# Two attention-fed mixture-of-experts layers: the last layer in groups of 512, 256 and 128 rows, and one routing product moved from GpSimd to VectorE

## The chip, the cores and the metric

The kernel runs on one NeuronCore of a Trainium2 chip. The metric is the device time of one execution in microseconds (us), lower is better. TensorE does the matmuls; VectorE (DVE), ScalarE (ACT) and GpSimd (POOL) do the elementwise work; SyncE (SP) issues most of the DMAs, GpSimd the indirect ones, which gather or scatter rows by a list of row numbers. Each engine works through its own list of instructions in order and waits on semaphores for the others.

## The reference

Inputs are q, k, v of shape (4, 8, 576, 64), and the weights of two expert layers. Cut to what matters:

```python
attn = softmax(block-causal mask of q @ k.T / sqrt(64)) @ v       # blocks of 64 positions
x = attn as (2304, 512)                                           # a row is a token
# first expert layer: 8 experts, each token goes to its two best
noisy = x @ w_gate + log1p(exp(x @ w_noise)) * noise
out[t] = sum over the two best e of weight * (relu(x[t] @ w1[e]) @ w2[e])   # 512 -> 1024 -> 512
# second expert layer: each token goes to its best expert alone
logits = out @ w_gate2 + modality_bias[modality_id]
e = argmax(logits); gate = softmax(logits)[e]
y[t] = gate * (relu(out[t] @ v1[e]) @ v2[e])                      # 512 -> 1024 -> 512
```

With the inputs given, the reference sends 1165 tokens of the second layer to expert 1, 1139 to expert 2 and none to the others. 866 and 852 of these do not use expert 7 in the first layer.

## The kernel before, in words

All matrices are float32 split into a high and a low part of a type that TensorE takes in one pass, so that each product is three matmuls: high by high, high by low, low by high. The weights come from memory as `raw` tiles of 128x1024, ScalarE copies the high part (`wh`), and VectorE or GpSimd subtracts it to make the low part (`wl`).

The program has three stages. **Attention** works over 16 pairs of heads. When a batch is complete, a part of the *first routing* (`route`, line 650) follows: it finds the two best experts of each token and makes, with matmuls of 0/1 matrices, the list of row numbers of each expert. `routes` runs it three times: for batches 0 and 1, for batch 2, and for batch 3. In it `hot_a` (line 281) makes the products `sl_ov` of a one-hot matrix with the values to be listed, `hot_b` the other one-hot matrix `sl_ob`, and `lists` (line 296) multiplies the two on TensorE into `pt`. The second run ends in `early(1)` (line 1135), which turns the sums into row numbers (`acc`, `ids`, `idg`) and issues the three gathers `wide<-X,idg` of the first expert-1 job.

The **first expert layer** is a list of jobs (`Job`, line 466). A job gathers tiles of 128 rows (`xr`), transposes them on TensorE into the one PSUM tile `px`, copies high and low parts to `xth` (ScalarE) and `xtl` (VectorE), runs `mm1` (the first matrix, `ph`, 96 matmuls as wide as the job's rows, up to 512) and then per tile of rows `mm2` (the second matrix, `py`, 24 matmuls of 512 columns). The transposes of the next job stand inside `mm2` of the present one. In attention's last microseconds TensorE already runs `mm1` of the first job (expert 0; there its tiles bear the names `ps` and `kh`), and its `mm2` holds the transposes of the expert-1 job, as `px<-ident,wide`. Rows of results are added to `X2`, and dot products with the second layer's gate (`zero<-py`, 8 per tile, VectorE) are added to `LG`.

The **last layer** needs the second routing, `gates(k)` (line 1466). `gates(0)` starts when the rows of experts 0 to 6 are in, and looks only at tokens that are complete by then; `gates(1)` starts when expert 7 is in and takes the rest. Each fills a table of row numbers. A table holds groups of 256 rows of one expert: three for `gates(0)` (`NE`), which takes only full groups, and seven for `gates(1)` (`NS`). Each group is one `Job` with its own load of both weight matrices. If a row finds no place, the flag `more` is 1 and a slow loop behind the list of jobs (line 1593) does what is left.

The order of instructions on TensorE, ScalarE and VectorE is fixed when the program is built. A planner keeps a modelled clock for each engine: during attention it picks the step that can start earliest (`earliest`, line 1316, due times in `SCHED`), and a routing step is let in when the modelled VectorE is free; a product on GpSimd makes the next routing step wait for the modelled GpSimd clock. In the expert stages `run` (line 1407) writes jobs in order and calls due routing steps between matmuls (`beat`, `tick`). Where a gather or a `wl` falls in a job is set there too: `fs` and `eb` say after which quarter of `mm1` a second-layer weight is split, and on which engine.

Of the kernel before, what the change touches and what calls it, by code (L numbers as in the profile page):

```python
# [30 lines left out]
def moe_kernel(tc, q, k, v, w_gate, w_noise, noise, w1, w2, mod_id, w_gate2, mod_bias, m2w1, m2w2, out):  # L31
    nc = tc.nc
    B, H, S, D = q.shape
    NT, DM = out.shape
    E = w_gate.shape[1]
# [3 lines left out]
    NP = CAP // 128  # L39

    FIRST = (2, 3)
    NE = 3
    NV = 5
    NA1 = E * NP
    NTT = NT // 128
    G2 = 256
    NG2 = 16
    NS = 10 - NE
    NA2 = NG2 * G2 // 128
    NQ = 4  # L50
    NY = 3
# [3 lines left out]
    def bc(ap, shape):  # L55
        return ap.to_broadcast(shape)
# [47 lines left out]
    with ExitStack() as top:  # L104
# [18 lines left out]
        def iota(t, pattern, base=0, cm=0):  # L123
            nc.gpsimd.iota(t, pattern=pattern, base=base, channel_multiplier=cm, allow_small_or_imprecise_dtypes=True)
# [34 lines left out]
                            for name, dt in (("ids0", I32), ("idg0", I32), ("gts0", F32)))  # L159
        gts1 = cst.tile([128, NA1], F32, name="gts1")  # L160

        table = [(cst.tile([128, 2 * n], I32, name="ids%d" % i), cst.tile([128, 2 * n], F32, name="gts%d" % i),
                  cst.tile([1, NG2 + 1], I32, name="eg%d" % i)) for i, n in ((2, NE), (3, NS), (4, NG2))]
        eo = cst.tile([1, NG2 + 1], I32, name="eo")
        gso = cst.tile([128, E], F32, name="gso")
        more = cst.tile([1, 1], I32, name="more")
# [22 lines left out]
        def consts2():  # L189
            iota(pad2, [[0, NA2]], base=NT + CAP, cm=1)  # L190
            iota(th2, [[G2, 9]])
            iota(th3, [[G2, 9]], base=G2 - 1)
            iota(th1, [[G2, 7]], base=CAP)
            nc.sync.dma_start(wg2, w_gate2.rearrange("(k p) e -> p k e", p=128))
            nc.sync.dma_start(mid, mod_id.bitcast(I32).rearrange("(p t w) -> p t w", p=128, w=2))
            gps.tensor_copy(midf, mid[:, :, 0])
            nc.sync.dma_start(bias1, mod_bias.rearrange("(o m) e -> o (m e)", o=1))
            nc.gpsimd.memset(one1, 1.0)
            gps.tensor_scalar(vals2[:, :, 0], bc(part, [128, NTT]), 1.0, None, op0=OP.add)
            gps.tensor_copy(vals2[:, :, 1], lane[:, 0:NTT])  # L200
# [265 lines left out]
        class Job:  # L466
# [44 lines left out]
            def mm1(s, f, hp_):  # L511
                wh, wl = (w[:, :, 128 * (f % 2):128 * (f % 2) + 128] for w in s.wa[f // 2])
                h1, h2 = hp_(f, s.n)
                for c0, cn in s.parts:
                    cs = slice(c0, c0 + cn)
                    ph = ps_h.tile([128, 512], F32, name="ph")
                    for kk in range(4):
                        for i, (w, xx) in enumerate(((wh, s.xth), (wh, s.xtl), (wl, s.xth))):
                            ten.matmul(ph[:, 0:cn], w[:, kk], xx[:, kk, cs], start=(kk == 0 and i == 0), stop=(kk == 3 and i == 2))
                        if kk % 2 == 0:  # L520
                            beat()
                    act.activation(h1[:, cs], ph[:, 0:cn], AF.Relu)
# [85 lines left out]
            return Job((w1[e], w2[e]), X1, nt, lambda t: ids1[:, e * NP + t0 + t:e * NP + t0 + t + 1],  # L608
                       lambda t: gts1[:, e * NP + t0 + t:e * NP + t0 + t + 1], add_rows(ids1, e * NP + t0, nt, then), need)

        def group(W1, W2, table, ev, ic, gc, emit, need=(None, None)):
            def w():
                e = ev()
                return W1[bass.ds(e, 1)].rearrange("o d f -> (o d) f"), W2[bass.ds(e, 1)].rearrange("o f d -> (o f) d")
            return Job(w, table, G2 // 128, ic, gc, emit, need)

        prev_out = []
        HG = 4
# [10 lines left out]
        def job2(k, g):  # L629
            ids, gts, eg = table[k]  # L630
            ic = lambda t: ids[:, 2 * g + t:2 * g + t + 1]
            j = group(m2w1, m2w2, X2, lambda: nc.sync.value_load(eg[0:1, g:g + 1], min_val=0, max_val=E - 1), ic,
                      lambda t: gts[:, 2 * g + t:2 * g + t + 1], put_rows(ic), ("eg%d" % k, "ids%d%d" % (k, g >= HG)))
            if k == 0:
                j.apart = last_rows
            return j
# [6 lines left out]
        chain = lambda k, p: lambda: walk(gates(k), now[0] + .5, p)  # L643
        firsts = [job1(0, FIRST[0], NP - FIRST[0], need=(None, "ids1"))]
        firsts += [job1(e, then={E - 2: chain(0, 1), E - 1: chain(1, 1)}.get(e), need=(None, "ids1")) for e in range(2, E)]
        seconds = [job2(0, g) for g in range(NE)] + [job2(1, g) for g in range(NS)]
        stage = Stage([j00, j10] + firsts + seconds)


        def route(b0, nb):  # L650
# [101 lines left out]
            for b in range(nb):  # L752
                n = slice(10 * b, 10 * b + 10)
                ob = yield from hot_b(rt, bl[:, n], 10)
                ov = yield from hot_a(rt, a[:, n], 10, 0, NA1, va[:, n], b0 + nb < B)
                yield from lists(pl, ob, ov, 10, b == 0, b == nb - 1)
            if b0 == 0:
                vec.tensor_copy(acc1, pl)
# [648 lines left out]
        def run(jobs, hp_, ea, eb, nxt=None, stage=stage):  # L1407
# [3 lines left out]
            for n, j in enumerate(jobs):  # L1411
                nx = jobs[n + 1] if n + 1 < len(jobs) else nxt

                def rows():
                    if nx and nx.ready(1) and len(nx.xr) < nx.nt:
                        nx.gather(len(nx.xr))

                for f in range(len(j.hh), NF // 128):
                    j.mm1(f, hp_)
                    if f in fs and len(j.wb) < NQ:  # L1420
                        stage.split(eb[fs.index(f) % len(eb)] if "ids1" in flags else vec)
                    stage.fetch(ah)
                    rows()
                    filler()
                    tick(j.n * .005)
# [40 lines left out]
        def gates(k):  # L1466
# [1 line left out]

            flags.add("chain")
            pool = r2[0]  # L1470
            th = th2 if k else th3
            ids, gts, dst = table[k]
            cap = ids.shape[1]
            sh = [128, NTT, E]
# [27 lines left out]
            n = yield from experts_of(pool, gn, gs, dst, "g_")  # L1502
            flags.add("eg%d" % k)
            if k == 1:

                go, s_ = yield from starts(pool, base, th1, "o_")
                vec.tensor_copy(gso, s_)
                yield .3
                no = yield from experts_of(pool, go, gso, eo, "o_")
                m = pool.tile([1, 1], F32, name="g_m")  # L1510
                vec.tensor_scalar(m, n, -float(NS), 0.0, op0=OP.add, op1=OP.max)
                yield .3
                vec.tensor_add(m, m, no)
                yield .3
                vec.tensor_scalar(more, m, 1.0, None, op0=OP.min)
                yield .3
# [10 lines left out]
            vec.scalar_tensor_tensor(a, st, float(G2 // 128), a, op0=OP.mult, op1=OP.add)  # L1527
            yield .3
            if k == 0:
                vec.tensor_tensor(t0, oh, bc(gn[:, None, :], sh), op=OP.mult)  # L1530
                yield .3
                vec.tensor_reduce(st, t0, axis=AX, op=OP.add)
                yield .3
                vec.scalar_tensor_tensor(msk, st, float(G2), pos, op0=OP.mult, op1=OP.is_gt)
                yield .3

            vec.tensor_scalar(msk, msk, -1e5, 1e5, op0=OP.mult, op1=OP.add)
            yield .3
# [2 lines left out]
            if k < 2:  # L1541
                new = tl("new") if k else placed
                vec.tensor_scalar(new, a, cap - .5, None, op0=OP.is_lt)
                yield .3
                if k:
                    vec.tensor_add(placed, placed, new)
                    yield .3

            vec.tensor_tensor(l, l, bc(mx[:, :, None], sh), op=OP.subtract)
# [26 lines left out]
        with sp():  # L1576
            with tc.tile_pool(name="hp1", bufs=1, reuse_waits="tile") as hp1:
                run([j00, j10, j11] + firsts, hidden(hp1), [gps], [gps], seconds[0])
            hp2 = ph2.enter_context(tc.tile_pool(name="hp2", bufs=1, reuse_waits="tile"))
            with tc.tile_pool(name="ws2", bufs=4, reuse_waits="tile") as ws2:  # L1580
                rings["raw"].add(ws2, 4)
                run(seconds, hidden(hp2), [vec], [vec, gps])
                while heap or fill:
                    if heap:
                        pop()
                    clk["pe"] = max(clk["pe"], clk["dve"], now[0]) + 1
                    filler()
            rings["raw"] = Ring("raw", F32, (wp, 5))
# [119 lines left out]
```

## Time and profile before

Three timed runs gave 990.72, 992.0 and 994.84 us (median 992.0).

| | |
|---|---|
| time of the profiled execution | 991.67 us |
| its span, first to last instruction | 989.9 us |
| mean granted TensorE clock | 0.993 |
| busy: TensorE / weight loads / VectorE / ScalarE / GpSimd | 96% / 87% / 71% / 53% / 53% |
| weight tiles of 512 KB (`raw`) | 144 |
| DMA traffic | 141.6 MB, mean 143 GB/s |

The profiled execution lies 0.3 us below the median, well within the spread, so that its rows can be added up against its own time. A matmul's record is longer than its share of TensorE, because matmuls overlap; the distance between two starts is what one of them costs.

### The profile page before, as it was taken

To read this page: it belongs to the slowest core of one execution; us is meant where nothing else is said; L and a number is where in the kernel's file an instruction comes from. 1 tells how busy PE (TensorE), PEld (TensorE's weight loads), DVE (VectorE), ACT (ScalarE), POOL (GpSimd) and SP (SyncE) were. 2 spreads that over 40 slices of the span, in tenths; PEclk is the share of its full clock that TensorE was granted. 3 is DMA by queue.
4 is the path that set the end of the run, shared out by engine and by line. 5 is a ranking of instruction groups with operands and counts; after the bars stand their busy time and mean duration, and the time that the engine had idled before them with its cause. 6 is when DMAs were issued, how large, how long until landed. Compare 5 with 4: busy or idle time off the path is not lost.

```text
span 989.9 us, 17527 instructions
## 1 busy us (share of the span) xinstructions
PE 949.4 (96%) x6072; PEld 860.7 (87%) x6072; DVE 703.6 (71%) x1707; ACT 520.9 (53%) x1156; POOL 521.0 (53%) x488
## 2 busy tenths in 40 slices
PE   8999998999979999999999999999999899999995
PEld 6989897998868998989899898989979779999994
DVE  6878779888769967386693948669788866555450
ACT  6989997988542344334333333433335535555551
POOL 6234333464423599586685848648476253333321
PEclk9999999999989999999999999999999999999998
DMA  5577752222376377464563727434466877776620
GB/s 127 106 217 197 221 131 65 72 60 68 92 236 197 54 171 181 118 151 107 128 129 93 143 86 150 107 86 54 143 129 195 279 234 233 229 220 219 197 86 12
DMA packets 158258, 141.60 MB, mean 143 GB/s; under 512 B 76233, under 2 KB 124745, under 8 KB 158034
## 3 DMA queue, kind: packets, MB, share of 16 engines
q1 hardware_dynamic: 139042, 106.92, 37.4%
q0 software_dynamic: 18064, 33.23, 16.7%
q8 instruction: 50, 0.82, 0.3%
q14 instruction: 46, 0.38, 0.1%
q10 hardware_dynamic: 1056, 0.26, 0.1%
HBM read 112.54 MB, written 28.36 MB: 142 GB/s over the span
## 4 chain that ended last, share of the span: by engine, by line
PE 73%; DVE 9%; issue 5%; ACT 5%; DMA 4%; POOL 3%; SPq 1%; POOLq 0%; ACTq 0%; DVEq 0%
PE ph L71 28%; PE py L71 27%; PE pt L71 7%; PE ps L71 6%; PE pa L71 3%; PE px L71 2%; DVE wl L71 2%; ACT p L71 2%; POOL wl L71 2%; ACT kp L71 1%; DVE kp L71 1%; DMA xr<-X,ids 1%; DVE nm L71 1%; DVE PTl L71 1%; DMA qld<-in_q_dram 1%
## 5 line engine op out<-in xcount | busy, mean ns | idle before, releaser
L71 POOL TENSOR_TENSOR wl<-raw,wh 128x1024 fp32r<-128x1024 f32 x80 | 207.5, 2623 | 106.4 <-ACT wh L71 92.2
L71 PE MATMUL ph<-xth,wh 128*128 128x320 f32 (+2 forms) x800 | 241.2, 302 | 2.1 <-DVE kp L71 2.1
L71 PE MATMUL ph<-xth,wl 128*128 128x320 f32 (+2 forms) x800 | 240.0, 300 | 0.0
L71 PE MATMUL ph<-xtl,wh 128*128 128x320 f32 (+2 forms) x800 | 240.0, 300 | 0.0
L71 DVE SCALAR_TENSOR_TENSOR zero<-py,gts,wide 128x512 f32<-128x512 f32 x304 | 227.5, 748 | 8.3
L71 PE MATMUL py<-wh,kp 128*128 128x512 f32 x496 | 168.1, 399 | 0.0
L71 PEld LDWEIGHTS ph<-xth,wh 128*128 128x128 f32 x800 | 151.7, 190 | 4.0 <-DVE kp L71 2.8
L71 PEld LDWEIGHTS ph<-xtl,wh 128*128 128x128 f32 x800 | 151.7, 190 | 0.7
L71 PEld LDWEIGHTS ph<-xth,wl 128*128 128x128 f32 x800 | 151.7, 190 | 0.0
L71 ACT ACTIVATE wh<-raw 128x1024 fp32r<-128x1024 f32 x144 | 150.8, 1053 | 0.6 <-DMA raw<-in_moe_w_dram 0.5
L71 ACT ACTIVATE yr<-py,gts 128x512 f32<-128x512 f32 x60 | 41.3, 689 | 147.1 <-PE py L71 104.6
L71 PEld LDWEIGHTS py<-wh,kp 128*128 128x128 f32 x496 | 94.0, 189 | 18.5
L71 DVE SCALAR_TENSOR_TENSOR hl<-ph,hh 128x320 fp32r<-128x320 f32 (+2 forms) x100 | 46.4, 465 | 79.1 <-ACT hh L71 78.9
L71 DVE TENSOR_TENSOR wl<-raw,wh 128x1024 fp32r<-128x1024 f32 x64 | 80.1, 1259 | 29.8 <-ACT wh L71 29.1
L71 PE MATMUL py<-wl,kp 128*128 128x512 f32 x248 | 97.4, 393 | 0.0
L71 PE MATMUL ps<-kh,kp 128*128 128x256 f32 (+5 forms) x320 | 95.7, 340 | 0.6 <-ACT p L71 0.4
L71 POOL DMA_INDIRECT xr<-X,ids x55 | 57.5, 1045 | 73.5 <-PE px L71 44.2
L71 PE MATMUL py<-wh,hh 128*128 128x512 f32 x232 | 94.0, 405 | 0.0
L71 DVE TENSOR_TENSOR xtl<-px,xth 128x512 fp32r<-128x512 f32 x58 | 40.0, 690 | 74.3 <-ACT xth L71 74.3
L71 PE MATMUL py<-wl,hh 128*128 128x512 f32 x232 | 90.6, 390 | 1.7 <-POOL wl L71 1.7
L71 ACT ACTIVATE hh<-ph 128x320 fp32r<-128x320 f32 (+2 forms) x100 | 41.8, 418 | 95.1 <-PE ph L71 91.6
L71 PE MATMUL py<-wh,hl 128*128 128x512 f32 x232 | 90.9, 392 | 0.0
(253 smaller groups left out, 1830.9 us busy)
## 6 DMA issues: line engine op xcount, KB each, us to landing
raw<-in_moe_w_dram SPq DMA_DIRECT2D x144, 512.0 KB, 4.0
X<-zero SPq DMA_DIRECT2D x13, 512.0 KB, 4.2
kld<-in_k_dram SPq DMA_DIRECT2D x32, 128.0 KB, 2.9
vld<-in_v_dram SPq DMA_DIRECT2D x32, 128.0 KB, 2.7
X<-x SPq DMA_DIRECT2D x16, 256.0 KB, 2.6
qld<-in_q_dram SPq DMA_DIRECT2D x30, 128.0 KB, 2.8
wide<-in_moe_w_dram SPq DMA_DIRECT2D x4, 512.0 KB, 6.5
wide<-WG2T POOLq DMA_DIRECT2D x1, 2048.0 KB, 10.2
```

The costliest lines, as they stand in the source:

```text
L71: return f(*a, **kw)
```

## The change

The last layer's groups become 512 rows wide (`GW`), two in each table, and the second table gets two small ones in addition, one of 256 rows and one of 128. `gates(1)` therefore works out, beside the number of full 512-row groups of each expert (`gn`), the groups of 256 that hold the rest (`nr`, `gm`, `gr`, table `egs`). `more` is now worked out from the number of rows placed. In a job of 128 rows `mm1` reads its columns twice, so that a matmul is 256 wide. In the first routing the products of the second run go to VectorE. In the job `firsts[0]` (the rest of expert 0) the last two of four second-matrix splits go to VectorE. The ring of raw weight tiles has 7 in place of 9 in the last layer.

```diff
-    NE = 3
+    GW = 512
+    BW, NW, NSM = GW // 128, 2, 2
...
-            iota(th3, [[G2, 9]], base=G2 - 1)
+            iota(th3, [[GW, 9]], base=GW - 1)
...
-                            ten.matmul(ph[:, 0:cn], w[:, kk], xx[:, kk, cs], start=(kk == 0 and i == 0), stop=(kk == 3 and i == 2))
+                            o, xx = ph[:, 0:cn], xx[:, kk, cs]
+                            if cn == 128:
+                                o, xx = ph[:, 0:2 * cn].rearrange("p (r c) -> p r c", r=2), bc(xx[:, None], [128, 2, cn])
+                            ten.matmul(o, w[:, kk], xx, start=(kk == 0 and i == 0), stop=(kk == 3 and i == 2))
...
-        seconds = [job2(0, g) for g in range(NE)] + [job2(1, g) for g in range(NS)]
+        seconds = [job2(k, g) for k in range(2) for g in range(NW)] + [job2(1, g, True) for g in range(NSM)]
...
-                ov = yield from hot_a(rt, a[:, n], 10, 0, NA1, va[:, n], b0 + nb < B)
+                ov = yield from hot_a(rt, a[:, n], 10, 0, NA1, va[:, n], b0 == 0)
...
+                eb_ = [gps, gps, vec, vec] if j is firsts[0] else eb
...
-                        stage.split(eb[fs.index(f) % len(eb)] if "ids1" in flags else vec)
+                        stage.split(eb_[fs.index(f) % len(eb_)] if "ids1" in flags else vec)
...
             if k == 1:
-
+                nr = pool.tile([128, E], F32, name="g_nr")
+                vec.scalar_tensor_tensor(nr, gn, -float(GW), pp[:, NTT], op0=OP.mult, op1=OP.add)
+                yield .3
+                gm, gr = yield from starts(pool, nr, th2, "q_")
+                yield from experts_of(pool, gm, gr, egs, "q_")
...
+                    ten.matmul(pm, ones, held, start=True, stop=True)
...
+                    vec.tensor_scalar(more, m, float(NT) - .5, None, op0=OP.is_lt)
...
-            with tc.tile_pool(name="ws2", bufs=4, reuse_waits="tile") as ws2:
-                rings["raw"].add(ws2, 4)
+            with tc.tile_pool(name="ws2", bufs=2, reuse_waits="tile") as ws2:
+                rings["raw"].add(ws2, 2)
```

The planner then writes another order. All that follows up to the second routing run is the same in both. **First place: VectorE at the end of attention**, where that run makes its lists. `kp<-ps` are the low parts of the first job's hidden rows, `kld` and `qld` halves of its weights. Before:

```order
L71 TENSOR_TENSOR sl_oa<-lane,sl_a_3856 128x400
L71 SCALAR_TENSOR_TENSOR kp_3954<-ps,kp_3954 128x256
L71 TENSOR_TENSOR wl<-kld,wh 128x512
L71 TENSOR_TENSOR wl<-qld,wh 128x512
L71 SCALAR_TENSOR_TENSOR kp_3954<-ps,kp_3954 128x256
L71 SCALAR_TENSOR_TENSOR kp_4041<-ps,kp_4041 128x256
```

and now:

```order
L71 TENSOR_TENSOR sl_oa<-lane,sl_a_3857 128x400
L71 SCALAR_TENSOR_TENSOR kp_3955<-ps,kp_3955 128x256
L71 TENSOR_TENSOR sl_ov<-sl_oa,vals 128x1000 x2
L71 TENSOR_TENSOR wl<-kld,wh 128x512
L71 TENSOR_TENSOR wl<-qld,wh 128x512
L71 SCALAR_TENSOR_TENSOR kp_3955<-ps,kp_3955 128x256
L71 TENSOR_TENSOR acc_98<-acc_98,pt 128x200
```

The two products are new on VectorE, and the sum `acc`, which stood behind all eight `kp` and all four pairs of `wl`, now stands behind two `kp` and one pair. Between it and `idg` stand two `kp` and one pair of `wl` that were ahead of it. On TensorE the ten `pt<-sl_ov,sl_ob` stood behind the last of the 96 `ps<-kh` and `ps<-kl` matmuls of the first job; now three stand behind 24 of these and seven behind 36, so that 60 come after them. The four `sl_ov` are gone from GpSimd's list, and its three gathers `wide<-X,idg` stand behind the same work as before.

**Second place: TensorE at the start of the last layer**, the end of expert 7's `mm2` and the first `mm1` of the last layer. Before:

```order
L71 MATMUL py<-wh,hl_8193 128x512
L71 MATMUL py<-wh,hh_8258 128x512
L71 MATMUL py<-wl,hh_8258 128x512
L71 MATMUL py<-wh,hl_8259 128x512
L71 MATMUL ph<-xth,wh 128x256
L71 MATMUL ph<-xtl,wh 128x256
```

and now:

```order
L71 MATMUL py<-wh,hl_8192 128x512
L71 MATMUL py<-wh,hh_8257 128x512
L71 MATMUL py<-wl,hh_8257 128x512
L71 MATMUL py<-wh,hl_8258 128x512
L71 MATMUL px<-ident,xr 128x128 x4
L71 MATMUL ph<-xth,wh 128x512
L71 MATMUL ph<-xtl,wh 128x512
```

The transposes of the fourth tile of rows stand right ahead of the matmuls that read it. Twelve `py` earlier, where one tile was transposed, two follow each other without work between:

```order
L71 MATMUL py<-wh,kp_8072 128x512
L71 MATMUL py<-wl,kp_8072 128x512
L71 MATMUL py<-wh,kp_8072 128x512
L71 MATMUL px<-ident,xr 128x128 x8
L71 MATMUL py<-wh,hh_8113 128x512
```

At the change from the first table to the second, 12 `py` stand between the last list matmul of the second table's first eight columns and the first `px` that needs them, where there were 24; in later jobs 12 or more `py` stand behind each `px`.

## Rows read from the trace of the kernel before

**Rows 1.** Waits of TensorE over the span: us in total, times, longest

```profile
PE px L71 <- DMA wide<-X,idg: 6.7, 1, 6.7
PE ph L71 <- DVE kp L71: 2.1, 3, 1.1
PE py L71 <- POOL wl L71: 1.7, 1, 1.7
PE pt L71 <- DVE sl_ov L71: 1.6, 1, 1.6
```

**Rows 2.** Busy time by window: PE, PEld, DVE, ACT, POOL, clock, DMA

```profile
248.00:300.00 52.00, 43.90 (x286) 40.38 (x285) 35.09 (x103) 23.96 (x50) 17.91 (x17) 0.93 0.56 172
340.00:380.00 40.00, 38.26 (x203) 34.20 (x202) 26.54 (x66) 18.86 (x27) 36.46 (x21) 1.00 0.62 148
738.00:820.00 82.00, 76.93 (x540) 69.10 (x540) 69.00 (x152) 42.00 (x66) 42.08 (x26) 1.00 0.75 232
820.00:955.00 135.00, 135.00 (x877) 122.96 (x876) 69.54 (x101) 74.43 (x115) 46.59 (x30) 1.00 0.67 207
```

**Rows 3.** Timeline of TensorE in the last layer: start us, us, instruction

```profile
737.58 0.28 PE L71 MATMUL ph<-xth,wh 128*128 128x256 f32 x1
...
863.14 0.28 PE L71 MATMUL ph<-xth,wh 128*128 128x256 f32 x1
...
874.65 0.40 PE L71 MATMUL py<-wh,kp 128*128 128x512 f32 x1
...
883.79 0.39 PE L71 MATMUL py<-wh,hh 128*128 128x512 f32 x1
...
886.51 0.28 PE L71 MATMUL ph<-xth,wh 128*128 128x256 f32 x1
...
978.82 0.39 PE L71 MATMUL py<-wh,hl 128*128 128x512 f32 x1
```

**Rows 4.** Timeline of TensorE at the end of attention

```profile
268.10 1.03 PE L71 MATMUL pt<-sl_ov,sl_ob 128*128 128x200 bf16 x10
...
278.58 1.11 PE L71 MATMUL px<-ident,wide 128*128 128x128 f32 x4 [6.67 <-DMA wide<-X,idg]
...
283.62 0.60 PE L71 MATMUL px<-ident,wide 128*128 128x128 f32 x4
...
286.82 0.60 PE L71 MATMUL px<-ident,wide 128*128 128x128 f32 x4
```

**Rows 5.** Timeline of GpSimd at the end of attention

```profile
256.34 4.42 POOL L71 TENSOR_TENSOR sl_ov<-sl_oa,vals 128x600 bf16<-128x600 bf16 x4
...
273.23 1.05 POOL L71 DMA_INDIRECT wide<-X,idg  x1 [9.78 <-DVE u L71]
```

**Rows 6.** Timeline of VectorE at the end of attention

```profile
255.91 0.41 DVE L71 SCALAR_TENSOR_TENSOR kp<-ps,kp 128x256 fp32r<-128x256 f32 x1
259.54 0.85 DVE L71 TENSOR_TENSOR wl<-kld,wh 128x512 fp32r<-128x512 f32 x1 [3.22 <-ACT wh L71]
...
270.78 0.35 DVE L71 TENSOR_TENSOR acc<-acc,pt 128x200 f32<-128x200 f32 x1
...
272.31 0.16 DVE L71 TENSOR_TENSOR idg<-gp,i 128x3 int32<-128x3 f32 x1
```

**Rows 7.** Products on VectorE in the other routings: ns least/median/most

```profile
L71 DVE TENSOR_TENSOR sl_ov<-sl_oa,vals x8: 430/479/1202, 302.3 to 817.7; 128x270 bf16<-128x270 bf16 x4, 128x1000 bf16<-128x1000 bf16 x2, 128x360 bf16<-128x360 bf16 x2
```

**Rows 8.** One tile's way before the last layer: TensorE, ScalarE, VectorE

```profile
730.98 0.66 PE L71 MATMUL px<-ident,xr 128*128 128x128 f32 x4 [1.85 <-DMA xr<-X,ids]
...
731.67 0.60 ACT L71 ACTIVATE xth<-px 128x512 fp32r<-128x512 f32 x1 [1.77 <-PE px L71]
...
732.30 0.69 DVE L71 TENSOR_TENSOR xtl<-px,xth 128x512 fp32r<-128x512 f32 x1 [1.58 <-ACT xth L71]
```

**Rows 9.** TensorE where the second table's first gather is awaited

```profile
802.02 0.24 PE L71 MATMUL pt<-sl_ov,sl_ob 128*128 128x40 bf16 x3
...
809.08 0.63 PE L71 MATMUL px<-ident,xr 128*128 128x128 f32 x4 [1.26 <-DMA xr<-X,ids]
```

More of the change, by code (lines that the diff above doesn't have):

```diff
@@ L47, in moe_kernel @@
     NG2 = 16
-    NS = 10 - NE
     NA2 = NG2 * G2 // 128
@@ L160, in moe_kernel @@
         gts1 = cst.tile([128, NA1], F32, name="gts1")
-        table = [(cst.tile([128, 2 * n], I32, name="ids%d" % i), cst.tile([128, 2 * n], F32, name="gts%d" % i),
-                  cst.tile([1, NG2 + 1], I32, name="eg%d" % i)) for i, n in ((2, NE), (3, NS), (4, NG2))]
+        table = [(cst.tile([128, n], I32, name="ids%d" % i), cst.tile([128, n], F32, name="gts%d" % i),
+                  cst.tile([1, NG2 + 1], I32, name="eg%d" % i)) for i, n in ((2, BW * NW), (3, BW * NW + 2 * NSM - 1), (4, 2 * NG2))]
+        egs = cst.tile([1, NG2 + 1], I32, name="egs")
         eo = cst.tile([1, NG2 + 1], I32, name="eo")
@@ L609, in job1, with group @@
                        lambda t: gts1[:, e * NP + t0 + t:e * NP + t0 + t + 1], add_rows(ids1, e * NP + t0, nt, then), need)
-        def group(W1, W2, table, ev, ic, gc, emit, need=(None, None)):
+        def group(W1, W2, table, ev, ic, gc, emit, need=(None, None), nt=G2 // 128):
             def w():
@@ L614, in w @@
                 return W1[bass.ds(e, 1)].rearrange("o d f -> (o d) f"), W2[bass.ds(e, 1)].rearrange("o f d -> (o f) d")
-            return Job(w, table, G2 // 128, ic, gc, emit, need)
+            return Job(w, table, nt, ic, gc, emit, need)
         prev_out = []
@@ L627, in put_rows, with job2 @@
             return put
-        def job2(k, g):
+        def job2(k, g, small=False):
             ids, gts, eg = table[k]
-            ic = lambda t: ids[:, 2 * g + t:2 * g + t + 1]
-            j = group(m2w1, m2w2, X2, lambda: nc.sync.value_load(eg[0:1, g:g + 1], min_val=0, max_val=E - 1), ic,
-                      lambda t: gts[:, 2 * g + t:2 * g + t + 1], put_rows(ic), ("eg%d" % k, "ids%d%d" % (k, g >= HG)))
+            c, n = (BW * NW + 2 * g, 2) if small else (BW * g, BW)
+            x = egs if small else eg
+            ic = lambda t: ids[:, c + t:c + t + 1]
+            j = group(m2w1, m2w2, X2, lambda: nc.sync.value_load(x[0:1, g:g + 1], min_val=0, max_val=E - 1), ic,
+                      lambda t: gts[:, c + t:c + t + 1], put_rows(ic), ("egs" if small else "eg%d" % k, "ids%d%d" % (k, c >= 2 * HG)),
+                      min(n, ids.shape[1] - c))
             if k == 0:
@@ L1470, in gates @@
             pool = r2[0]
-            th = th2 if k else th3
+            th = th3 if k < 2 else th2
             ids, gts, dst = table[k]
@@ L1501, in gates @@
             gn, gs = yield from starts(pool, pp[:, NTT], th, "g_")
-            n = yield from experts_of(pool, gn, gs, dst, "g_")
+            yield from experts_of(pool, gn, gs, dst, "g_")
             flags.add("eg%d" % k)
             if k == 1:
+                nr = pool.tile([128, E], F32, name="g_nr")
[3 more added lines that the diff above has]
+                yield from experts_of(pool, gm, gr, egs, "q_")
+                flags.add("egs")
+                vec.tensor_scalar(gr, gr, 2.0, float(BW * NW), op0=OP.mult, op1=OP.add)
+                yield .3
+                vec.scalar_tensor_tensor(gr, gn, -float(BW), gr, op0=OP.mult, op1=OP.add)
+                yield .3
+                vec.tensor_add(nr, gs, gn)
+                yield .3
+                vec.tensor_scalar(nr, nr, NW + .5, 1e5, op0=OP.is_gt, op1=OP.mult)
+                yield .3
+                vec.tensor_add(gs, gs, nr)
+                yield .3
                 go, s_ = yield from starts(pool, base, th1, "o_")
@@ L1508, in gates @@
                 yield .3
[L1509 to L1516, printed above, removed]
+                yield from experts_of(pool, go, gso, eo, "o_")
             t0, pos, st = tl("t0", sh), tl("pos"), tl("st")
@@ L1526, in gates @@
             a, bl = yield from row_col(pool, pos, NTT)
-            vec.scalar_tensor_tensor(a, st, float(G2 // 128), a, op0=OP.mult, op1=OP.add)
-            yield .3
-            if k == 0:
+            if k < 2:
+                w = msk if k == 0 else tl("w")
+                s2 = tl("s2")
                 vec.tensor_tensor(t0, oh, bc(gn[:, None, :], sh), op=OP.mult)
                 yield .3
-                vec.tensor_reduce(st, t0, axis=AX, op=OP.add)
+                vec.tensor_reduce(s2, t0, axis=AX, op=OP.add)
                 yield .3
-                vec.scalar_tensor_tensor(msk, st, float(G2), pos, op0=OP.mult, op1=OP.is_gt)
+                vec.scalar_tensor_tensor(w, s2, float(GW), pos, op0=OP.mult, op1=OP.is_gt)
                 yield .3
+            if k == 1:
+                vec.tensor_tensor(t0, oh, bc(gr[:, None, :], sh), op=OP.mult)
+                yield .3
+                vec.tensor_reduce(s2, t0, axis=AX, op=OP.add)
+                yield .3
+                vec.scalar_tensor_tensor(st, st, float(BW), s2, op0=OP.mult, op1=OP.subtract)
+                yield .3
+                vec.tensor_tensor(st, st, w, op=OP.mult)
+                yield .3
+                vec.tensor_add(st, st, s2)
+                yield .3
+            vec.scalar_tensor_tensor(a, st, (float(BW), 1.0, float(G2 // 128))[k], a, op0=OP.mult, op1=OP.add)
+            yield .3
             vec.tensor_scalar(msk, msk, -1e5, 1e5, op0=OP.mult, op1=OP.add)
@@ L1546, in gates @@
                     vec.tensor_add(placed, placed, new)
+                    yield .3
+                    held = tl("held", dt=BF16)
+                    vec.tensor_copy(held, placed)
+                    yield "pe", 0
+                    pm = ps_r.tile([128, NTT], F32, name="pt")
+                    ten.matmul(pm, ones, held, start=True, stop=True)
+                    yield .4
+                    m = pool.tile([1, 1], F32, name="g_m")
+                    vec.tensor_reduce(m, pm[0:1], axis=AX, op=OP.add)
+                    yield .3
+                    vec.tensor_scalar(more, m, float(NT) - .5, None, op0=OP.is_lt)
                     yield .3
```

## The prediction

> **What bounds the kernel now.** I read the table of busy time first: TensorE is busy for 96% of the span, VectorE for 71%, so time can be won in two ways only, by giving TensorE less to do or by ending one of its waits. Then the list of TensorE's waits [rows 1]: the longest by far is 6.67 us for the gather of the first expert-1 rows; the others that the change touches are 1.7 us for a weight split on GpSimd and about 2 us for low parts in the last layer. Then the windows [rows 2]: from 820 to 955 TensorE has 135.00 of 135 us busy, so the last layer is bound by TensorE alone; from 738 to 820 it has 76.93 of 82. From 248 to 300 the granted clock is 0.93, elsewhere 1.00.
>
> Last, the timelines. In the last layer [rows 3] the starts give the price of a matmul: 96 of `mm1` with 256 columns from 863.14 to 874.65, (874.65 − 863.14)/96 = 0.120 us each; 12 of `mm2` with 512 columns from 883.79 to 886.51, 2.72/12 = 0.2267 us each (0.227 below). The `mm2` of two tiles with its 48 `py` and two `px` sets takes 886.51 − 874.65 = 11.86, so one `px` set of four transposes is (11.86 − 48 × 0.2267)/2 = 0.49. The whole layer lasts from 737.58 to 978.82 + 0.39 = 979.21: 241.6 us.
>
> The sum below is made against the profiled execution, 991.67 us, 0.3 below the median of the runs shown.
>
> **First part: the lists of the second routing.** Now GpSimd makes the four `sl_ov` from 256.34 to 260.76 [rows 5], but the ten list matmuls run only at 268.10 [rows 4], since the planner put them behind the whole `mm1` of the first job. `acc` follows at 270.78, `idg` at 272.31 [rows 6], the gather is issued at 273.23 [rows 5] and TensorE goes on at 278.58, 5.35 us after the issue. It had waited since 271.91.
>
> The change adds two products of 128x1000 to VectorE. In the other routings those of 270 to 1000 elements take 430 to 1202 ns [rows 7]; I take 1.2 us each, 2.4 us together. Before the first `wl` at 259.54 VectorE idles for 3.22 us [rows 6], so they lie in that idle time. If the cover were gone they would push the low parts behind them by 2.4 us. The last list matmul now stands 60 `mm1` matmuls earlier, 60 × 0.12 = 7.2 us, so the lists end near 269.1 − 7.2 = 261.9 and `acc` runs near 262. The order then puts two `kp` (0.41 each) and two `wl` (0.85 each) between `acc` and `idg`, with the 1.5 us of small steps that separate them now: `idg` is due near 265.7, the gather 0.9 later at 266.6, and data 5.35 later at 271.95. TensorE arrives at 271.91. The wait of 6.67 goes almost whole. What is late next is the same gather, by a few tenths, if anything.
>
> The clock comes with it. Behind the wait the stretch from one `px` to the next, 278.58 to 283.62, lasts 5.04 us, and the next one, 283.62 to 286.82, of the same work, 3.20 [rows 4]; the window's granted clock of 0.93 [rows 2] says that part of it ran at 1.2 instead of 2.4 GHz, after TensorE had idled. Without the wait I take these 1.84 us off too. Term: −6.67 − 1.84 = **−8.5**. Bounds: −8.5, and −3 if products, splits or gather come 5 us late together (the splits wait for ScalarE's `wh`, which I can't move on paper).
>
> **Second part: two splits of `firsts[0]` on VectorE.** TensorE's 1.7 us wait for `wl` on GpSimd [rows 1] lies in the stretch from 340 to 380, where GpSimd is busy for 36.46 us of 40 and VectorE for 26.54 [rows 2]. VectorE has 13.5 us free there and two splits of a 128x1024 tile, at twice the 0.85 of the 128x512 ones [rows 6], ask for 3.4. Term: **−1.7**, bounds 0 and −1.7; without that cover it would be a wait for VectorE of the same size.
>
> **Third part: the work of the last layer.** By the reference's counts each expert has one full group of 512 in the first table (866 and 852 complete rows). The rest is 1165 − 512 = 653 and 1139 − 512 = 627, which gives one more group of 512 each and leaves 141 and 115: one group of 256 and one of 128. So ten groups of 256 (20 tiles) become 4 × 512 + 256 + 128 (19 tiles).
>
> Before: 10 × (11.51 + 48 × 0.227) = 10 × 22.4 = 224, and 18 × 0.49 = 8.8 for the transposes, 232.7. Now a 512 group takes 96 × 0.227 + 96 × 0.227 = 43.58; four are 174.3. The 256 group is 22.4. The 128 group reads its columns twice, so its `mm1` is priced as a 256 one, 11.51, and with 24 × 0.227 it takes 16.95. With 17 `px` sets (two more stand inside the entry) the sum is 222.0. Term: **−10.7**. About 5.9 of it is the tile that is gone (24 `py` and a `px`), and 5.0 is 384 times the difference between two 256 matmuls and one of 512, 0.240 − 0.227 = 0.013. That an `mm1` of 512 columns costs what an `mm2` of 512 costs is the one assumption; it has the same form and the same weight load per matmul. Bounds: +5.0 if it costs two of the 256 ones. A doubled read of columns stands nowhere in the trace: from 0 to 96 × (0.227 − 0.120) = +10.3 if it costs as much as 512 columns; I take 0, since the number of columns streamed is the same as in rows 3.
>
> The Trainium skill speaks against the 5.0: "TensorE: Matmul & The Clock Gate", section "Back-to-back issue gap", gives N/2.4 + 2.5 ns for an isolated matmul at the fast clock, hence 109 and 216 ns, a gain of 2.6 ns per pair and 1.0 us in all; the sum would be 976. The same section gives about 131 ns for 512 columns in a sustained stream, by which the gain would be many times mine. The trace has 0.120 and 0.227 [rows 3] in a stretch without waits and agrees with neither; the rows decide.
>
> Fewer loads (6 instead of 10, 48 instead of 80 raw tiles) relieve ScalarE, VectorE and the DMA queues, none of which bounds the layer; so I give them nothing, and the smaller `raw` ring costs nothing for the same reason.
>
> **Fourth part: the waits of the last layer.** Of its 241.6 us, 8.9 are not in the 232.7: some 3.8 are matmuls of the routing, which stay; 5.1 are waits (1.26 in rows 9, 1.6 for `sl_ov` and up to 2.1 for `kp` in rows 1).
>
> At the entry two `px` sets now follow each other without work between, with a single `px` tile: the second waits for ScalarE's `xth`, 0.60, and VectorE's `xtl`, 0.69, of the first [rows 8], some 1.4 with the semaphores; and the fourth set stands right ahead of the `mm1` that reads it, where another 1.1 goes for the same two copies (the first matmul needs only `xth`). **+2.5**; from 1.3, if the pair is partly covered, to 4.5 if the gather is late as now (1.85 in rows 8). While TensorE waits there, ScalarE's and VectorE's later work waits behind these very copies, nothing else.
>
> At the second table, lists end near 802.1 and the data are there at 809.08, 7.0 us later [rows 9]. Before, 24 `py` covered 24 × 0.227 = 5.45 of it; now 12 do, 2.73. The wait would grow from 1.26 to 4.0; I take 3, since VectorE's small steps between list and gather no longer stand behind as many low parts. Bounds 1 and 9: `gates(1)` has some 30 more small operations on VectorE, at about 0.2 us each (`idg` takes 0.16 [rows 6]) 6 us in all. They have two groups of 512, 87 us, to hide beside, where there were three of 256, 70 us; without that cover they are the wait.
>
> With 1 us for the other places the waits come to 6.5, where there were 5.1: **+1.4**. The layer is then 241.6 − 10.7 + 1.4 = 232.3, a term of **−9.3**. The last results' way out is the same.
>
> **Sum:** 991.67 − 8.5 − 1.7 − 9.3 = 972.2, forecast **972**.
>
> **The rivals.**
>
> *The first wait stays.* GpSimd issues the gather in its own order, behind the same work as before; if that work, or ScalarE's `wh` ahead of the splits, keeps the gather near 273, the 8.5 are not won: 980.7. For it: the order gives only places, and GpSimd reaches the gather after a wait of 9.78 for VectorE [rows 5], so it has been idle, which speaks against it.
>
> *The second table comes late.* The 6 us of added steps are not hidden: 972.2 + 6 = 978. For it: a chain of small operations on one engine, in order; against it: VectorE's 70 busy us of 135 [rows 2].
>
> *Wide `mm1` gains nothing:* 972.2 + 5.0 = 977. Against it: the cadence in rows 3.
>
> *The added waits don't come,* since the planner's order leaves the tiles' copies time: 972.2 − 2.5 − 3 = 966.7. Against it: one `px` tile.
>
> *Slower: a row finds no place.* The 128 group has room for 128 rows and by the reference 115 are left, 13 to spare. If noise in the kernel's own products moves more than 13 rows (the point from which it decides), `more` is 1, and the loop behind the jobs runs at least one group of 256, nothing of it beside other work: 23.4 (a period of rows 3, 886.51 − 863.14) and 5.35 for the gather, 972.2 + 28.8 = 1001. Against it: the kernel's parts keep float32 products nearly whole.
>
> **How the numbers follow.** Chances: the forecast 0.63, the first wait stays 0.12, the second table late 0.10, no gain from wide `mm1` 0.05, waits vanish 0.07, the fallback 0.03. The forecast's own range is 967 to 978 (first part up to 5.5 less, waits 2 less to 3 more). The range 965 to 982 takes in the rivals up to 980.7 and leaves out the fallback and combinations of two. A change within 0.5%, about 5 us, can't be told from none. Faster than 987 are all cases but the fallback: 0.93, after 0.04 for combinations (the doubled read at +10.3 on top of a first wait that stays gives 991); these are split between same, 0.03, and slower, 0.04 with the fallback.
>
> **What would show it.** Right: no wait of TensorE for `wide<-X,idg` near 272, or under 1 us, and a granted clock of 1.0 there; `idg` near 266; no wait for GpSimd's `wl` near 370; starts of 512-wide `ph` 0.227 apart and of the doubled ones 0.120; two waits at the entry of the last layer that sum to about 2.5, one of about 3 at the second table; a layer of some 232 us. Wrong: `acc` still behind 268; `ph` 0.240 apart; a gap behind the first table's second group; a loop behind the last job.

## The result and the profile after

The changed kernel takes 983.14 us in the median of 4 runs (981.37 to 985.97), the kernel before 992.26 beside it: ratio 0.990, 95% interval 0.9862 to 0.9939. In the first batch of experiments the same kernel gave 980.48 (0.9885, 0.9869 to 0.9900). The forecast was 972, with a range from 965 to 982: the sign was right, but half of the gain is missing.

The profiled execution took 985.97 us, span 984.2. Five distances between starts on TensorE show where its 5.7 us come from. The last column is a second execution of the same kernel, 983.49 us, profiled in the experiments.

| stretch on TensorE | before | after | after, again |
|---|---|---|---|
| start to first `py` of the first job | 268.91 | 270.90 | 269.04 |
| to first `ph` of the expert-1 job (first hand-over) | 21.99 | 14.40 | 13.69 |
| `firsts[0]`: its first `ph` to that of the next job | 37.48 | 35.46 | 35.43 |
| expert 7: first `py` to first `ph` of the last layer (entry) | 31.49 | 44.43 | 41.71 |
| last layer, to the end of its last `py` | 241.63 | 229.49 | 232.27 |

In the first execution the last layer is some 12 us shorter, and the 31 us ahead of it are 13 longer; in the second the two are 9 and 10. The five changes of the first execution sum to −6.8; 0.7 comes back in the expert-1 job's `mm1`, and some 0.4 elsewhere. The first 2 us belong to attention, where the order is the same in both; the second execution doesn't have them.

TensorE's waits after, in the form of [rows 1], those that the change touches:

```profile
PE px L71 <- DMA xr<-X,ids: 6.2, 3, 2.9
...
PE pt L71 <- DVE sl_ov L71: 3.4, 1, 3.4
PE px L71 <- DVE xtl L71: 2.7, 2, 1.4
PE pt L71 <- DVE g_held L71: 1.6, 1, 1.6
...
PE ph L71 <- ACT xth L71: 0.9, 1, 0.9
```

The 6.7 us for `wide<-X,idg` and the 1.7 for GpSimd's `wl` are gone. In their place the list has waits for `sl_ov`, for rows (`xr`), for `xtl` and `xth`, and for a count (`g_held`).

The first hand-over, answering to [rows 4 to 6]: VectorE's new products, `acc` and `idg`, GpSimd's gather, and the three `px` of TensorE.

```profile
258.29 2.30 DVE L71 TENSOR_TENSOR sl_ov<-sl_oa,vals 128x1000 bf16<-128x1000 bf16 x2
263.98 0.36 DVE L71 TENSOR_TENSOR acc<-acc,pt 128x200 f32<-128x200 f32 x1 [0.79 <-PE pt L71]
267.93 0.15 DVE L71 TENSOR_TENSOR idg<-gp,i 128x3 int32<-128x3 f32 x1
268.84 1.06 POOL L71 DMA_INDIRECT wide<-X,idg  x1 [3.84 <-DVE lg L71]
273.65 0.60 PE L71 MATMUL px<-ident,wide 128*128 128x128 f32 x4
276.87 0.60 PE L71 MATMUL px<-ident,wide 128*128 128x128 f32 x4
281.48 0.66 PE L71 MATMUL px<-ident,wide 128*128 128x128 f32 x4 [1.24 <-DVE xtl L71]
```

Less the 2 us of attention, `idg` comes near 266 and the gather near 266.9, as forecast; the first `px` doesn't wait, and the next follows 3.22 us later, where 3.20 was the stretch at full speed. A new wait of 1.24 for `xtl` stands at the third.

Windows of after, as in [rows 2]; the last two are the entry:

```profile
248.00:300.00 52.00, 48.36 (x323) 44.18 (x324) 44.05 (x117) 28.49 (x59) 13.96 (x14) 1.00 0.61 199
340.00:380.00 40.00, 40.00 (x212) 35.88 (x212) 33.77 (x71) 20.36 (x30) 36.78 (x22) 1.00 0.71 192
706.00:719.00 13.00, 9.56 (x38) 7.14 (x37) 12.70 (x22) 1.38 (x2) 5.48 (x3) 0.74 0.52 132
719.00:745.00 26.00, 20.16 (x92) 15.10 (x92) 16.01 (x44) 6.24 (x9) 19.95 (x16) 0.93 0.62 141
```

The granted clock near 272 is 1.00 now, and it is 0.74 from 706 to 719. TensorE there:

```profile
707.30 0.39 PE L71 MATMUL py<-wh,kp 128*128 128x512 f32 x1
711.12 0.28 PE L71 MATMUL pt<-sl_ov,sl_ob 128*128 128x40 bf16 x3 [3.44 <-DVE sl_ov L71]
...
711.81 0.63 PE L71 MATMUL py<-wl,hh 128*128 128x512 f32 x1
712.24 0.63 PE L71 MATMUL py<-wh,hl 128*128 128x512 f32 x1
...
730.34 0.66 PE L71 MATMUL px<-ident,xr 128*128 128x128 f32 x4 [1.70 <-DMA xr<-X,ids]
735.40 0.63 PE L71 MATMUL px<-ident,xr 128*128 128x128 f32 x4 [1.63 <-DMA xr<-X,ids]
737.44 1.04 PE L71 MATMUL px<-ident,xr 128*128 128x128 f32 x4 [1.41 <-DVE xtl L71]
...
743.77 0.51 PE L71 MATMUL ph<-xth,wh 128*128 128x512 f32 x1 [0.88 <-ACT xth L71]
744.49 0.50 PE L71 MATMUL ph<-xtl,wh 128*128 128x512 f32 x1 [0.22 <-DVE xtl L71]
```

The lists of `gates(0)` wait 3.44 us, and behind them a 512-column matmul costs 712.24 − 711.81 = 0.43 us in place of 0.227, the 1.2 GHz level, until 716.91: twelve `py` cost some 2.4 us more than at 2.4 GHz. In the second execution eight do, some 1.6 us. Then each of the four `px` or its reader waits once. The timeline of VectorE at 707, without the dot products, and then that of GpSimd (start, us, instruction):

```profile
707.04 4.02 DVE L71 TENSOR_TENSOR sl_ov<-sl_oa,vals 128x360 bf16<-128x360 bf16 x1
716.92 0.53 DVE L71 TENSOR_TENSOR sl_ov<-sl_oa,vals 128x360 bf16<-128x360 bf16 x1
```

GpSimd:

```profile
706.02 2.28 POOL L71 DMA_INDIRECT X<-yr,ids  x1 [0.69 <-ACT yr L71]
707.76 2.90 POOL L71 TENSOR_TENSOR wl<-raw,wh 128x1024 fp32r<-128x1024 f32 x1
...
726.09 1.02 POOL L71 DMA_INDIRECT xr<-X,ids  x1 [0.30 <-issue]
727.14 2.38 POOL L71 TENSOR_TENSOR wl<-raw,wh 128x1024 fp32r<-128x1024 f32 x1
729.68 1.00 POOL L71 DMA_INDIRECT xr<-X,ids  x1 [0.16 <-issue]
```

The same product takes 4.02 us the first time and 0.53 the second. The long one ends at 711.06, which is 0.4 behind the end of GpSimd's `wl` (707.76 + 2.90 = 710.66), nearly as if it had begun only then. This `wl` splits the first matrix for the last layer's first job. Another such split stands between the first gather and the second, but it stood there before the change too, and the second `px` didn't wait. What differs in this execution is the landing: the second gather's rows come 5.6 us after its issue, where it was 4.0 before and 4.1 in the second execution, in which this `px` waits 0.33. Why they land later here isn't shown.

VectorE stands in the same way elsewhere in this trace, at no cost: a weight split of `firsts[0]` on VectorE takes 4.54 us from 360.09, where 1.22 is usual, beside two splits on GpSimd that last to 363.54, and TensorE doesn't wait for it.

The last layer itself, answering to [rows 3]: the first `ph`, the 256-row job, the 128-row job, the last `py`.

```profile
743.77 0.51 PE L71 MATMUL ph<-xth,wh 128*128 128x512 f32 x1 [0.88 <-ACT xth L71]
...
933.22 0.28 PE L71 MATMUL ph<-xth,wh 128*128 128x256 f32 x1
...
944.73 0.40 PE L71 MATMUL py<-wh,kp 128*128 128x512 f32 x1
...
956.11 0.28 PE L71 MATMUL ph<-xth,wh 128*128 128x256 f32 x1
...
967.62 0.40 PE L71 MATMUL py<-wh,kp 128*128 128x512 f32 x1
...
972.87 0.39 PE L71 MATMUL py<-wh,hl 128*128 128x512 f32 x1
```

The `mm1` of 256 rows and that of 128 doubled rows both take 11.51 us, 0.120 per matmul, as priced.

### The profile page after: what moved, and what is told of

The parts are those of the page before. It is cut to its first block, busy times and chain, and to the rows that moved or that the text cites. A ratio compares the mean times of both kernels' runs of the same rounds, so it can differ in the third digit from the quotient of the medians.

```text
span 984.2 us, 16351 instructions
## 1 busy us (share of the span) xinstructions
PE 941.2 (96%) x5661; PEld 835.9 (85%) x5661; DVE 684.8 (70%) x1676; ACT 484.2 (49%) x1090; POOL 489.7 (50%) x472
## 4 chain that ended last, share of the span: by engine, by line
PE 68%; issue 11%; DVE 7%; ACT 5%; POOL 5%; DMA 2%; POOLq 0%; SPq 0%; ACTq 0%; DVEq 0%
PE ph L71 25%; PE py L71 25%; PE pt L71 8%; PE ps L71 6%; PE pa L71 3%; POOL wl L71 2%; PE px L71 2%; ACT p L71 2%; DMA xr<-X,ids 1%; DVE nm L71 1%; DVE PTl L71 1%; DVE wl L71 1%; DMA raw<-in_moe_w_dram 1%; ACT kp L71 1%; DVE kp L71 1%
## 5 line engine op out<-in xcount | busy, mean ns | idle before, releaser
L71 POOL TENSOR_TENSOR wl<-raw,wh 128x1024 fp32r<-128x1024 f32 x70 | 181.9, 2617 | 111.9 <-ACT wh L71 109.4
L71 PE MATMUL ph<-xth,wh 128*128 128x320 f32 (+3 forms) x672 | 217.9, 324 | 2.1 <-DVE kp L71 1.2
L71 PE MATMUL ph<-xtl,wh 128*128 128x320 f32 (+3 forms) x672 | 217.2, 323 | 0.2 <-DVE xtl L71 0.2
L71 PE MATMUL ph<-xth,wl 128*128 128x320 f32 (+3 forms) x672 | 217.1, 323 | 0.0
L71 PEld LDWEIGHTS ph<-xth,wh 128*128 128x128 f32 x672 | 126.6, 188 | 8.3 <-DVE kp L71 1.9
L71 PEld LDWEIGHTS ph<-xth,wl 128*128 128x128 f32 x672 | 126.5, 188 | 5.0
L71 ACT ACTIVATE wh<-raw 128x1024 fp32r<-128x1024 f32 x112 | 117.8, 1052 | 1.5 <-DMA raw<-in_moe_w_dram 1.3
L71 DVE SCALAR_TENSOR_TENSOR hl<-ph,hh 128x320 fp32r<-128x320 f32 (+4 forms) x84 | 43.4, 519 | 80.0 <-ACT hh L71 79.9
L71 ACT ACTIVATE hh<-ph 128x320 fp32r<-128x320 f32 (+4 forms) x84 | 38.7, 461 | 100.9 <-PE ph L71 99.6
L71 ACT ACTIVATE p<-ps,nm 128x288 f32<-128x288 f32 (+8 forms) x160 | 79.3, 501 | 9.6 <-DVE nm L71 8.7
```

Source lines behind the costliest of these rows:

```text
L71: return f(*a, **kw)
```

## The experiments

The theory after these readings: the first two parts give what was forecast; the last layer saves its 12 us too, and gives them back at the entry, above all because the wider `sl_ov` meets a GpSimd split and one of the two engines must stand still. Each ratio is against the kernel before, beside which it ran.

**The changed kernel once more**, called the control below. 

> The changed kernel once more. Theory (the lists of gates(0) lose to a split on GpSimd): VectorE's sl_ov of 128x360 again takes about 4 us where its twin takes 0.53, TensorE waits about 3.4 us for it, and the time is 983 within 3. Rival (the stall was an accident of one execution): sl_ov takes about 0.5, no wait there, and the time is about 977 to 980.

Measured 980.48 us (0.9885). `sl_ov` took 4.02 us again and TensorE waited 3.34 for it:

```profile
704.39 4.02 DVE L71 TENSOR_TENSOR sl_ov<-sl_oa,vals 128x360 bf16<-128x360 bf16 x1
708.47 0.24 PE L71 MATMUL pt<-sl_ov,sl_ob 128*128 128x40 bf16 x3 [3.34 <-DVE sl_ov L71]
```

The stall isn't an accident: it is in every profile of this order.

**The first two parts alone**, in the kernel before:

```diff
-                ov = yield from hot_a(rt, a[:, n], 10, 0, NA1, va[:, n], b0 + nb < B)
+                ov = yield from hot_a(rt, a[:, n], 10, 0, NA1, va[:, n], b0 == 0)
...
+                eb_ = [gps, gps, vec, vec] if j is firsts[0] else eb
```

> The kernel before with the first two parts of the change alone: products of the second routing on VectorE, two splits of firsts[0] on VectorE; the last layer in groups of 256 as before. Theory: these two parts give 7 to 10 us, so 983 to 985, as much as the whole change, because the last layer gives back at its entry what its matmuls save. Rival (the prediction's sum with the attention stage slower): the last layer does save 9, and this kernel stays near 982 + 9 = 991.

Measured 981.85 us (0.9903, 0.9888 to 0.9919), as much as the whole change. In the profile the first hand-over is 8.1 us shorter, `firsts[0]` 2.05, and the lead of 9.5 us then stays to the end.

**The third part alone**, the two edits above undone in the changed kernel:

> The changed kernel without the first two parts: the last layer in groups of 512, 256 and 128, products and splits on GpSimd as before. Theory: matmul work of the last layer 12 us less, its entry 12 us more, so 992 within 3. Rival (the prediction's sum): 992 - 9 = 983.

Measured 989.77 us (0.9978, 0.9966 to 0.9989). So groups of 512 won 2 us by themselves: in the profile the last layer is 12.3 us shorter than before and the entry 8.8 longer. The entry has the stall again: `sl_ov` 4.02, wait 3.33.

**One split moved off GpSimd.**

```diff
+                ea_ = [gps, vec, gps, gps] if nx is seconds[0] else ea
...
-                            stage.split(ea[left[1] % len(ea)] if "ids1" in flags else vec)
+                            stage.split(ea_[left[1] % len(ea_)] if "ids1" in flags else vec)
```

> The changed kernel, but the second of the four first-matrix splits made for the first job of the last layer is on VectorE, not on GpSimd; it stands there three dot products behind the sl_ov that took 4.02 us. Theory (the two engines shut each other out): sl_ov takes 0.5 us, TensorE's wait of 3.44 for it goes, and with it most of the 2.8 us at the lower clock behind it: 977 to 979. Rival (sl_ov is slow by itself, or its wait is covered by the next one, for the gather): sl_ov at 4 us or the waits for xr longer by as much, 982 to 984.

Measured 978.47 us (0.986, 0.9842 to 0.9878). VectorE, in that profile, and GpSimd's scatter of rows beside it:

```profile
703.86 2.17 POOL L71 DMA_INDIRECT X<-yr,ids  x1 [0.80 <-ACT yr L71]
704.77 0.53 DVE L71 TENSOR_TENSOR sl_ov<-sl_oa,vals 128x360 bf16<-128x360 bf16 x1
707.48 1.22 DVE L71 TENSOR_TENSOR wl<-raw,wh 128x1024 fp32r<-128x1024 f32 x1
```

The product is short again, and TensorE doesn't wait for the lists. The scatter, which ran ahead of the split in the control too, doesn't hold the product up: it is the split that does. The entry shrinks from 41.71 (the control) to 37.08; 0.9 of the gain goes to a longer wait for the first rows (2.47 for 1.53). The profiled spans differ by 4.6 us (977.1 and 981.7), the medians by only 2.0, with intervals that overlap, so the time alone doesn't size this effect well; the next run does.

**A wider table in the kernel before.** `NE = 4` for `NE = 3` in the kernel of the first two parts: groups of 256, no job of 512.

> The kernel before with the first two parts of the change, its last layer in groups of 256 as before, and four such groups in the first table instead of three (six in the second in place of seven). Work and order of GpSimd ahead of the lists are the same; the one thing that grows there is sl_ov on VectorE, from 128x270 to 128x360, some 0.09 us. Theory (the wider table alone makes sl_ov miss its gap ahead of the split on GpSimd, whatever the groups): sl_ov takes about 4 us, TensorE waits over 3 us for it and runs at the lower clock behind it, 6 us more than with three groups, 987 to 989. Rival (the collision needs the 512-row groups and their order): sl_ov about 0.5 us, 982.

Measured 986.64 us (0.995, 0.9936 to 0.9963), 4.8 more than with three groups. The timelines of VectorE and GpSimd with three groups:

```profile
704.29 0.44 DVE L71 TENSOR_TENSOR sl_ov<-sl_oa,vals 128x270 bf16<-128x270 bf16 x1
705.02 2.97 POOL L71 TENSOR_TENSOR wl<-raw,wh 128x1024 fp32r<-128x1024 f32 x1
```

With four, and TensorE's lists behind them:

```profile
704.28 4.03 DVE L71 TENSOR_TENSOR sl_ov<-sl_oa,vals 128x360 bf16<-128x360 bf16 x1
705.00 2.91 POOL L71 TENSOR_TENSOR wl<-raw,wh 128x1024 fp32r<-128x1024 f32 x1
708.37 0.24 PE L71 MATMUL pt<-sl_ov,sl_ob 128*128 128x40 bf16 x3 [3.59 <-DVE sl_ov L71]
```

Both products start at the same time. That of 270 columns ends 0.29 us before the split's recorded start, and that of 360 would have ended 0.2 before it (0.53 after 704.28); the profile calls its spans on GpSimd rough. The narrow one slips through, the wide one stands until the split is over; the split takes 2.9 to 3.0 us in either case. In all eight profiles that have this split on GpSimd its record starts 0.71 to 0.74 us behind that of `sl_ov`, while the scatter ahead of it starts 0.92 to 1.17 before `sl_ov`: the split keeps step with VectorE, so the meeting recurs. What ties the two isn't shown. The last layer's first `ph` comes 5.8 us later, of which 1.4 are won back at the second table. The rival, that the 512-row groups and their order are needed, falls.

**All four splits on VectorE** (`ea_ = [vec]`). 

> The changed kernel with all four first-matrix splits for the first job of the last layer on VectorE, none on GpSimd. Theory (exclusion of the two engines): the cast of vals that took 2.3 us takes 0.2, sl_ov 0.5, no gather stands behind a split: TensorE's waits for sl_ov and for the second gather go, 974 to 978. Rival: the splits of 1.2 to 1.7 us each stand in VectorE's order ahead of the lists, and the lists are late for them: 979 to 981.

Measured 983.43 us (0.9919, 0.9905 to 0.9932): my theory's number was wrong, and the time is above the rival's too. `sl_ov` and the cast are short, and the lists aren't late, which was the rival's reason, but TensorE now waits 3.56 us for dot products queued behind the splits:

```profile
726.17 0.79 PE L71 MATMUL py<-wh,kp 128*128 128x512 f32 x1 [3.56 <-DVE zero L71]
```

**More banks for the transposes of the entry**, with the second split on VectorE:

```diff
-                            nx.cols(left[0])
+                            nx.cols(left[0], ps_h if nx is seconds[0] and left[0] in (2, 3) else None)
...
-                            if left[2] >= nx.nt - left[0]:
+                            if left[2] >= nx.nt - left[0] and not (nx is seconds[0] and left[2] == 1):
```

> The last kernel (second split on VectorE) and, at the entry of the last layer, the third and fourth sets of transposes beside the second, written to banks of ph, which stand empty there, in place of the one px tile. Theory (the entry's waits come of the one tile and of the fourth set's place right ahead of its readers): the wait of 1.41 for xtl and those of 0.88 and 0.22 ahead of ph go, 2 to 3.5 us in all, so 975 to 977. Rival (the rows aren't there yet, the gather is what ends last): the wait moves to xr, and 978 stays.

Measured 975.83 us (0.9842, 0.9824 to 0.9860).

```profile
723.74 0.66 PE L71 MATMUL px<-ident,xr 128*128 128x128 f32 x4 [2.41 <-DMA xr<-X,ids]
727.34 0.63 PE L71 MATMUL px<-ident,xr 128*128 128x128 f32 x4 [0.17 <-DVE zero L71]
728.30 0.66 PE L71 MATMUL ph<-ident,xr 128*128 128x128 f32 x4 [0.34 <-DMA xr<-X,ids]
729.42 0.65 PE L71 MATMUL ph<-ident,xr 128*128 128x128 f32 x4 [0.46 <-DMA xr<-X,ids]
732.67 0.39 PE L71 MATMUL ph<-xth,wh 128*128 128x512 f32 x1
```

The waits of 1.41, 0.88 and 0.22 have become 0.34 and 0.46; the entry takes 34.53 us.

**The count of placed rows later.** The matmul on `g_held`, its sum and `more` stand at the end of `gates(1)`, behind the second table. 

> The changed kernel with the count of placed rows (one matmul of g_held, its sum and the flag) moved behind the second table. Theory (the matmul stands in TensorE's order ahead of its operand): the wait of 1.6 us for g_held goes, and the second table's gather comes no later: 978 to 980. Rival (the time is given back at the next wait, for the second table's rows): 980 to 981.

Measured 978.22 us (0.986, 0.9846 to 0.9875), 2.3 less than the control, with intervals that just overlap: the wait is gone, two new ones of 0.32 and 0.67 for the table's `sl_ov` have come, and the second table's rows are awaited 1.40 us instead of 2.84 in the control.

**One read in the 128-row job.** `if cn == 64:` for `if cn == 128:`. 

> The changed kernel without the doubled read in the job of 128 rows: its 96 matmuls of the first matrix read 128 columns once. Theory (the prediction took 0.120 us each for the doubled form, and the trace shows that): half the columns cost from 0.06 to 0.12 us, so the job is up to 5.8 us shorter, 975 to 981. Rival (a matmul of so few columns costs more than one of 256, which would be what the doubling is for): 96 times the excess longer, above 983.

Measured 981.80 us (0.9894, 0.9880 to 0.9908), no difference from the control (0.9885, 0.9869 to 0.9900). The first `ph` and the first `py` of that job:

```profile
953.45 0.22 PE L71 MATMUL ph<-xth,wh 128*128 128x128 f32 x1
...
964.12 0.45 PE L71 MATMUL py<-wh,kp 128*128 128x512 f32 x1
```

That is 10.67/96 = 0.111 us for 128 columns, against 0.120 for 256: the doubled read costs 0.8 us at most, and saves nothing here.

**Three edits together:** second split on VectorE, banks for the transposes, the count later. 

> The three edits together: second split on VectorE, third and fourth transposes in banks of ph, the count of placed rows behind the second table. Theory (three separate waits of one engine): 975.8 less the 2.3 of the last edit, 972 to 975, which is the prediction's sum. Rival (they share a cause, so one makes up for the other): 976.

Measured 972.08 us (971.34 to 972.42; 0.9807, 0.9793 to 0.9820), 1.9% below the kernel before, and below the changed one. Its entry takes 34.40 us and its last layer 228.07.

## Why the prediction was wrong

*First part, −8.5:* right. The hand-over is 7.6 and 8.3 us shorter in the two executions, 8.1 with the parts alone; the products took 1.15 us each. A wait for `kp` in the expert-1 job's `mm1` (0.92) takes some 0.7 back. (Two of its sums are a little off: the rows add up to 266.05 for `idg`, not 265.7, and the trace has 265.94 when attention's 2 us are taken off; 5 us late would leave −3.5, not −3.) *Second part, −1.7:* right, −2.0.

*Third part, −10.7 of matmul work:* right. The `mm1` of 512 columns goes at 0.227, the doubled one at 0.120, no row was left over. Without the entry's share (2.5 of waits and 0.98 for two `px` sets) the forecast for the last layer was −12.8; it is −12.1 in the first execution, −12.3 with this part alone, and −9.4 in the second execution, where the granted clock behind the second table's wait was lower (0.92 from 820 to 850).

*Fourth part, the entry:* this step failed. I put down +2.5 with the bounds 1.3 and 4.5, and 0.98 of work; measured are +12.9 and +10.2. The parts that I named came as priced: 1.41 between the pair, 0.88 and 0.22 ahead of `ph`. What I didn't price is ahead of them: the prediction has no term for the lists of `gates(0)`, which stand in expert 7's `mm2` (its "matmuls of the routing, which stay" are those inside the last layer), though the diff widens the first table from 6 columns to 8 and with it `sl_ov` from 128x270 to 128x360. Its own cost is 0.09 us. But on the other engine a split starts within 0.3 us of its end, and so it costs 3.4 us of wait and some 2.4 of lower clock in the first execution, 3.3 and 1.6 in the second. The moved split and the wider table in the old last layer show this cause from both sides. Most of the rest are the waits for the second rows, 1.63 in one execution and 0.33 in the other, and a second stretch at 1.2 GHz behind the third `px` (`py` 0.43 apart from 738.70 to 740.83 in the first execution), some 1.6 in either; these are read from the traces, and no run tests them alone.

The trace of before had such a stall, and none of my rows shows it, a cast of 128x18 on VectorE beside a split on GpSimd:

```profile
709.76 2.39 POOL L71 TENSOR_TENSOR wl<-raw,wh 128x1024 fp32r<-128x1024 f32 x1 [7.51 <-ACT wh L71]
709.85 2.35 DVE L71 CAST vals<-g_t 128x18 bf16<-128x18 f32 x1
```

I bounded products by their own durations in [rows 7] and never asked what ran beside them. The Trainium skill has the rule ("SBUF — State Buffer", section "Who interferes with whom"): a VectorE instruction with two inputs in SBUF contends with a GpSimd instruction that reads SBUF; and it says of the ports that the two share, that whoever issues first holds them for the whole instruction while the other blocks. The trace agrees that one engine stands until the other is through: `sl_ov` and `wl` both read two SBUF tiles, and 4.02 us is the time to the split's end and 0.4 more. It doesn't bear out who comes first: by the records `sl_ov` starts 0.72 us ahead of the split, and yet it is `sl_ov` that stands. With GpSimd's spans rough, no run here shows when the ports are taken. The cast reads one tile alone, so the rule for two inputs doesn't cover it.

*The other waits:* I gave "1 us for the other places"; `g_held` alone is 1.6. Of the 2.1 for `kp` that I put into the last layer of before, 0.4 lie in the first expert layer. The second table's wait was forecast as 3 and is 2.87.

*The range:* the upper end, 982, covered one failed part at a time. No rival had a collision of two engines ahead of the entry; I priced delays by adding operations up in order, which can't give 4 us for 0.5. With the three edits the time is the forecast's, 972; that doesn't make the forecast right, since those edits aren't in the change. Nor does the rival of 980.7, though the control came out at 980.48: its first wait did go, so the nearness is chance.

## What to carry to other kernels

When an instruction on VectorE grows, look at what GpSimd starts just behind its end, 0.2 to 0.3 us here: a tenth of a microsecond more can cost the whole of the other engine's instruction, and the lower clock behind TensorE's wait as well. Price a hand-over from the first changed instruction on any engine, not from the first changed matmul. And a gain in matmul time that doesn't show in the total is found by comparing distances between the same two starts in both traces, stage by stage.

## What the runs showed of the hardware that was not expected

A cast of 128x18, 0.2 us when free, took 2.28 to 2.43 us whenever it met a split on GpSimd; with `NE = 4` the subtraction ahead of it met the split and took 2.42 in place of 0.18, and the cast was free. A wait of TensorE of 3.44 us was followed by 1.2 GHz (twelve `py` 0.43 us apart), one of 1.70 at 730.34 by none. A matmul of 128 columns costs 0.111 us, one of 256 costs 0.120, one of 512 costs 0.227: in this kernel there is hardly anything to save from 256 columns down to 128.
